# A first weight tile loaded and multiplied in two column halves, and two warm-up products less

## The chip, the cores and the metric

The kernel runs on one core of a Trainium2 chip. The metric is the time of the device for one execution, in microseconds (us). Three runs of the kernel before took 393.03, 393.30 and 393.21 us, median 393.21 us. Beside them there is one profiled execution with its trace.

## The reference

The input x has 2048 tokens of 448 numbers. Three parts are computed from it and mixed:

```python
# attention: 16 heads of 28, each token looks at 8 tokens, 2 apart, itself included
q, k, v = split(x @ wqkv)                       # 448 -> 3 * 448
a = softmax(q . k[s - 2 * (0..7)] * 28 ** -0.5) . v @ wo
# MLP
h = x @ w1 + b1;  h = max(h, 0);  b = (h * h) @ w2 + b2      # 448 -> 1792 -> 448
# gate
g = sigmoid((x * gate_w).sum(-1))
out = g * a + (1 - g) * b
```

All of it is float32. The kernel gets the accuracy on TensorE by splitting each operand into a high part (rounded to the matmul's format, names ending in `h`) and a low part (what the rounding left, names ending in `l`), and adds three products for each pair of tiles: high weights with high x, low weights with high x, and high weights with low x.

## The kernel before, in words

The tokens are worked in four chunks of 512. For each chunk TensorE makes the q, k and v projections (lines 430 to 467), whose 448 input rows are cut into three row tiles of 128 (k = 0, 1, 2) and a rest of 64. A column of the gate vector is appended to q's weights, twice, so that q's weights are 450 columns wide and the gate's sum falls out of the same products. The first hidden tiles of the MLP, the MLP's second product, and the output projection follow on TensorE, while GpSimd and VectorE work on the attention beside it.

The change touches the start of the kernel alone, and one constant of its planner. At the start:

- TensorE runs 18 products with a tile of zeros (`WARM`, line 816), which have no use for the result.
- ScalarE issues the loads of x's first row tile of chunk 0 in two halves of 256 tokens (line 823). SyncE issues all other loads in the order of lines 824 to 838: q's row tile 0 (128 x 450, one transfer, line 826), q's row tile 1, x's row tile 1, q's and x's row tile 2, the rest of q and k in two transfers of 64 rows, x's rest, and then k's and v's weights.
- ScalarE and VectorE make the high and low parts (lines 840 to 858). For k = 0, ScalarE makes the high part of the weights' first 225 columns (line 846) and VectorE that of the other 225 (line 847); VectorE then makes the high part of the first half of x (line 848), the low part of the weights, second half first (line 850), and the low part of x's first half (line 854). x's second half follows (lines 853 and 854).
- `qkv_first` (line 430) makes chunk 0's products. For k = 0 it takes the token tiles 0 and 1 (the first half of x) before the tiles 2 and 3. For each it goes through the three products j = 0 (high with high), 1 (low weights), 2 (low x), so that the first six products of the kernel are: high-high for tiles 0 and 1, low weights for tiles 0 and 1, low x for tiles 0 and 1.

In SBUF the high and low weights of q stand as two blocks of 225 columns, 226 apart. A product reads them woven, one column of each block in turn (`woven`, line 191), so that each product of 450 columns needs both blocks. The order of the columns in the accumulator is undone when ScalarE moves it out (line 373); the gate's column is read on its own (line 379).

What follows the start is written out by a planner. It holds a clock for TensorE (`plan.t`) and for each other engine, and emits each job of ScalarE, VectorE, GpSimd and SyncE in the order in which it expects the job to be able to start. TensorE's clock begins at `START` = 4850 ns (line 861) and is moved on by `FIRST` for the three row tiles of the first products; the other engines' clocks and the due times of the loads after the start are constants that do not depend on `START`.

Of the kernel before, what the change touches and what calls it, by code (L numbers as in the profile page):

```python
# [9 lines left out]
AF = mybir.ActivationFunctionType  # L10
# [3 lines left out]
S, D, H, DH, W, F = 2048, 448, 16, 28, 8, 1792  # L14
# [6 lines left out]
C = HG * DH  # L21
NF = F // P
CH = 512
NQ = D + 2
NH = D // 2 + 1
NG = NH + 1
# [6 lines left out]
MM448, MM512 = 189.2, 216.0  # L33
PE_LAT = 175.0
LAT = 60.0
START = 4850.0
ORDER = (3, 0, 1, 2)
WARM = 18
FIRST = (2700.0, 2350.0, 2300.0)
PP_BUFS = 4  # L40
ST_BUFS = 3
# [6 lines left out]
ACT, DVE, POOL, SYNC = "ACT", "DVE", "POOL", "SP"  # L48
# [8 lines left out]
class Plan:  # L57
# [30 lines left out]
    def add(self, eng, cost, fn, *deps, prio=MID, at=0.0, port=False, move=None):  # L88
        j = Job()
        j.eng, j.cost, j.fn, j.deps, j.prio, j.port, j.move = eng, cost, fn, [d for d in deps if d], prio, port, move  # L90
        j.at, j.done, self.count = max(at, self.now), None, self.count + 1
        j.n = self.count
        self.jobs[eng].append(j)
        return j
# [90 lines left out]
def gated_mix_kernel(ctx: ExitStack, tc: tile.TileContext, xT, wqkv, w1, w2, wo, b1, b2, out):  # L185
    nc = tc.nc
# [4 lines left out]
    def woven(w):  # L191

        if w.shape[1] in (NQ, NQ + 1):
            n = NH if w.shape[1] == NQ else D // 2
            return bass.AP(tensor=w.tensor, offset=w.offset, ap=[list(w.ap)[0], [1, n], [NG, 2]])
        return w.rearrange("p (i n) -> p n i", i=2)
# [9 lines left out]
    def woven_out(pt, n):  # L206
        return (pt[:, :2 * NH] if n == NQ else pt[:, :n]).rearrange("p (n i) -> p n i", i=2)

    def unwoven(t):
        return t.rearrange("p (n i) -> p i n", i=2)  # L210

    plan = Plan()
    add, need, event = plan.add, plan.need, plan.event
# [29 lines left out]
    zt, gt, g1t = zg[:, 0:2], zg[:, 2:4], zg[:, 4:6]  # L243
# [63 lines left out]
    ap = actx.enter_context(tc.tile_pool(name="phase_a", bufs=1, reuse_waits="tile"))  # L307
# [22 lines left out]
    class Acc:  # L330


        def __init__(self, tag, name, n, todo=None, now=True):
            self.ring, self.n, self.tag, self.name = rings[tag], n, tag, name
            self.all = self.todo = todo or 21
            self.rows, self.after = None, tuple(self.ring.take())
            if now:
                need(*self.after)
                self.open()
# [4 lines left out]
    def side_by_side(*todo):  # L344
        assert len(todo[0]) == len(todo[1])
        for pair in zip(*todo):
            need(*(j for e in pair for j in (*e[0].after, *e[3:])))
            for r, (acc, a, w, *_) in enumerate(pair):
                rows = slice(r * 64, r * 64 + 64)
                assert acc.rows in (None, r)  # L350
                nc.tensor.matmul(woven_out(acc.pt, acc.n), a[rows], woven(w[rows]), start=acc.todo == acc.all, stop=acc.todo == 1)  # L351
                acc.todo, acc.rows, acc.after = acc.todo - 1, r, ()
            plan.pe(MM512 if pair[0][0].n == CH else MM448 + (pair[0][0].n - D) * 1.7)

# [7 lines left out]
    def qkv_evacuate(acc, c, tl, b):  # L362
        par, t = c // 2, (c % 2) * 4 + tl
        pt, ready = acc.pt, plan.after_pe()
        first = (b, t // 2) not in stage
        if first:
            stage[b, t // 2] = [None, st_ring.take(), []]
        st = stage[b, t // 2]

        def evacuate():  # L370
            if first:
                st[0] = xap.tile([P, G, 2, C], F32, tag="stage", name=f"st{c}_{tl}_{b}", bufs=ST_BUFS)
            nc.scalar.activation(st[0][:, :, t % 2].rearrange("p (i g) c -> p i g c", i=2),  # L373
                                 unwoven(pt[:, :D]).rearrange("p i (g c) -> p i g c", c=C), AF.Copy)

        jobs = [add(ACT, 540.0, evacuate, ready, *st[1], *st[2], prio=SOON)]
        st[2].append(jobs[0])
        if b == 0:
            jobs.append(add(ACT, 165.0, lambda: nc.scalar.activation(zt[:, par, t:t + 1], pt[:, D + 1:D + 2], AF.Copy),
                            jobs[0], prio=SOON))  # L380
            z_jobs[par].append(jobs[1])
        acc.ring.give(*jobs)
        if not first:
            stage.pop((b, t // 2))
            t0 = t - t % 2
            dst, off = ((q_d, 0), (k_d, HALO), (v_d, HALO))[b]
            dd = dst[par, :, off:off + SP].rearrange("g (p s) c -> p g s c", s=NS)[:, :, t0:t0 + 2]
            j = dma(lambda: nc.sync.dma_start(dd.rearrange("p g s c -> p g (s c)"),
                                              st[0].rearrange("p g s c -> p g (s c)")), 512, 896, *st[2], prio=SOON)
            stores[b, par].append(j)  # L390
            st_ring.give(j)
# [24 lines left out]
    def accs(c, b, tls, tags):  # L416
        return [Acc(t, f"qkv{c}_{tl}_{b}", ncols(b)) for t, tl in zip(tags, tls)]
# [12 lines left out]
    def qkv_first(x):  # L430
        four = range(4)
        q = accs(0, 0, four, "bbbb")
        for k in range(3):
            todo = [full(x, q[i], i, 0, (k,)) for i in four]
            for some in ((0, 1), (2, 3)) if k == 0 else (four,):
                for j in range(3):
                    for i in some:
                        acc, a, w, *_ = todo[i][j]
                        nc.tensor.matmul(woven_out(acc.pt, NQ), a, woven(w), start=k == j == 0, stop=False)  # L439
            plan.pe(FIRST[k])  # L440
        for acc in q:
            acc.todo = 3
        k = accs(0, 1, four, "mmmm")
        t = [sum((last(x, a[i], i, b) for i in four), []) for b, a in ((0, q), (1, k))]
        f = [full(x, k[i], i, 1) for i in four]
        run(0, [t[0] + f[0] + f[1] + f[2] + f[3], t[1] + f[2] + f[3] + f[0] + f[1]],
            [(3, [(0, 0, q[0])], (k[0], k[0])),
             (12, [(0, i, q[i]) for i in (1, 2, 3)], (k[1], k[1])),
             (24, [], (k[0], k[2])), (33, [], (k[1], k[3])),
             (39, [(1, 0, k[0]), (1, 2, k[2])]), (48, [(1, 1, k[1]), (1, 3, k[3])])])  # L450
        v = accs(0, 2, four, "bbbb")
        f, l = [full(x, v[i], i, 2) for i in four], [last(x, v[i], i, 2) for i in four]
        run(0, [f[0] + l[0] + f[2] + l[2] + f[1] + f[3], f[1] + l[1] + f[3] + l[3] + f[0] + f[2]],
            [(15, [], (v[0], v[1])), (24, [], (v[2], v[3])),
             (33, [(2, 0, v[0]), (2, 1, v[1])]), (42, [(2, 2, v[2]), (2, 3, v[3])])])
# [359 lines left out]

    for _ in range(WARM):
        nc.tensor.matmul(warm[:, :2 * P].rearrange("p (i n) -> p i n", i=2), zero, zeros, start=True, stop=True)  # L817

    raws = [rawp.tile([P, 4, 512], F32, tag="raw", name="wqraw0")]
# [3 lines left out]
        nc.scalar.dma_start(rx[:, 0, cols], xT[0, :, 0, cols])  # L823
    for k in range(4):
        if k < 3:
            nc.sync.dma_start(raws[0][:, k, :NQ], wqkv[0, :, k])
        else:
            for b, rows in ((0, slice(0, 64)), (1, slice(64, P))):
                nc.sync.dma_start(raws[0][rows, k, :NQ], wqkv[b, rows, k])
        if k:  # L830
            nc.sync.dma_start(rx[:, k], xT[0, :, k])
    for b, tag in ((1, "k"), (2, "v")):
        raw = attp.tile([P, 3, D], F32, tag=tag, name=f"wqraw{b}")
# [6 lines left out]
    for k in range(3):  # L840
        wh, wl, raw = apart(wqh[:, k]), apart(wql[:, k]), in_a_row(raws[0][:, k])
        if k:
            nc.scalar.activation(wh, raw, AF.Copy)
            nc.vector.tensor_sub(wl, raw, f32(wh))
        else:
            nc.scalar.activation(wh[:, 0], raw[:, 0], AF.Copy)
            nc.vector.tensor_copy(wh[:, 1], raw[:, 1])
            nc.vector.tensor_copy(x.h[0][:, halves[0]], rx[:, 0, halves[0]])
            for i in (1, 0):
                nc.vector.tensor_sub(wl[:, i], raw[:, i], f32(wh[:, i]))  # L850
        for n, cols in enumerate(halves if k == 0 else (slice(0, CH),)):
            if k or n:
                nc.scalar.activation(x.h[k][:, cols], rx[:, k, cols], AF.Copy)
            nc.vector.tensor_sub(x.l[k][:, cols], rx[:, k, cols], f32(x.h[k][:, cols]))
# [5 lines left out]

    plan.t, plan.wire = START, 15000.0
    plan.now = 9800.0
# [119 lines left out]
    c = ORDER[0]  # L982
# [252 lines left out]
    rows = wo_d.rearrange("(i b) n -> i b n", b=14)  # L1235
# [31 lines left out]
    for g in range(2, 2 * NF):  # L1267
        i, f = g // (NF // 2), g % (NF // 2) * 2
        c = ORDER[i]
# [44 lines left out]
        st = at_hand() if last or wo_ready else None  # L1314
# [9 lines left out]
    for n, (tls, second) in enumerate(((left, False), (right, False), (left, True), (right, True))):  # L1324
        if second:
            o_turn(c, f, tls)
        if n in (1, 2, 3):
            st = at_hand()
# [51 lines left out]
```

## Time and profile before

| | us |
|---|---|
| runs: median (lowest, highest) | 393.21 (393.03, 393.30) |
| profiled execution: span from its first to its last instruction | 391.0 |
| median of the runs less this span | 2.2 |
| TensorE products / weight loads busy | 386.5 / 385.2 |
| VectorE / ScalarE / GpSimd busy | 261.4 / 205.4 / 260.6 |
| warm-up products, start of the first to the end of the last | 0.79 to 4.97 |
| first product with data starts | 5.01 |

The profiled execution has no time of its own beside its span; what lies around the span is taken as the difference to the median of the runs, 2.2 us. In the profile, PE is TensorE's products and PEld its weight loads, DVE is VectorE, ACT is ScalarE, POOL is GpSimd and SP is SyncE; a `q` after an engine's name is its queue of issued transfers. In a row of the timeline the first number is the start in us from the span's start, the second the time until the end of the last of the row's instructions; then come engine, line, operation, output <- input, shape and count, and in brackets the idle time of the engine before and what ended it. The names `wqraw` and `xraw` are the loaded float32 tiles of weights and x, `wqh`/`wql` the high and low weights, `qkv` an accumulator in PSUM. The recorded spans of products overlap, since products are pipelined; the distance between starts says how fast they follow one another.

### The profile page before, as it was taken

To read this page: it belongs to the slowest core of one execution; us is meant where nothing else is said; L and a number is where in the kernel's file an instruction comes from. 1 tells how busy PE (TensorE), PEld (TensorE's weight loads), DVE (VectorE), ACT (ScalarE), POOL (GpSimd) and SP (SyncE) were. 2 spreads that over 40 slices of the span, in tenths; PEclk is the share of its full clock that TensorE was granted. 3 is DMA by queue.
4 is the path that set the end of the run, shared out by engine and by line. 5 is a ranking of instruction groups with operands and counts; after the bars stand their busy time and mean duration, and the time that the engine had idled before them with its cause. 6 is when DMAs were issued, how large, how long until landed. Compare 5 with 4: busy or idle time off the path is not lost.

```text
span 391.0 us, 9273 instructions
## 1 busy us (share of the span) xinstructions
PE 386.5 (99%) x3828; PEld 385.2 (99%) x3828; DVE 261.4 (67%) x348; ACT 205.4 (53%) x501; POOL 260.6 (67%) x165
## 2 busy tenths in 40 slices
PE   9999999999999999999999999999999999999996
PEld 8999999999999999999999999999999999999995
DVE  4525523588685778778656989789666686668454
ACT  4757866362566566445555445345716343456740
POOL 0000002988999989959999887999998979661000
PEclk9999999999999999999999999999999999999999
DMA  7999999997174062654203779655635120226835
GB/s 236 400 355 302 382 376 350 378 370 246 49 246 157 1 219 80 220 171 161 90 2 137 242 183 296 208 124 141 213 111 173 78 96 2 88 63 164 143 107 188
DMA packets 64841, 73.75 MB, mean 189 GB/s; under 512 B 32480, under 2 KB 57632, under 8 KB 64416
## 3 DMA queue, kind: packets, MB, share of 16 engines
q1 hardware_dynamic: 64368, 72.79, 57.2%
q8 instruction: 30, 0.49, 0.5%
q10 hardware_dynamic: 432, 0.38, 0.3%
q14 instruction: 11, 0.09, 0.1%
HBM read 45.71 MB, written 28.25 MB: 189 GB/s over the span
## 4 chain that ended last, share of the span: by engine, by line
PE 99%; DVE 0%; DVEq 0%; issue 0%
PE b L351 33%; PE h L351 32%; PE qkv L351 23%; PE a L351 7%; PE qkv L439 2%; PE warm L817 1%; PE a L1170 1%; DVE bt_b L1053 0%; DVEq L1375 0%
## 5 line engine op out<-in xcount | busy, mean ns | idle before, releaser
L549 POOL TENSOR_TENSOR pp<-q,k 128x896 f32<-128x896 f32 x56 | 116.9, 2124 | 75.1 <-DMA k<-k_d 64.4
L561 POOL TENSOR_TENSOR pp<-lg,v 128x896 f32<-128x896 f32 x64 | 113.8, 1870 | 9.6 <-DVE o L571 5.3
L351 PE MATMUL h<-x,w1h 64*128 64x512 f32 x672 | 116.6, 376 | 0.0
L351 PE MATMUL qkv<-wqh,x 64*128 64x448 f32 (+1 forms) x528 | 82.2, 349 | 0.0
L553 DVE TENSOR_REDUCE lg<-pp 128x32 f32<-128x896 f32 x64 | 66.9, 1076 | 13.9 <-POOL pp L549 13.9
L351 PEld LDWEIGHTS h<-x,w1h 64*128 64x128 f32 x672 | 74.1, 186 | 0.0
L803 DVE TENSOR_TENSOR h<-h,h 128x512 fp32r<-128x512 f32 x56 | 38.6, 690 | 52.4 <-ACT h L802 52.3
L351 PE MATMUL h<-x,w1l 64*128 64x512 f32 x336 | 69.3, 376 | 0.0
L351 PE MATMUL b<-w2bh,h 64*128 64x448 f32 x448 | 67.8, 349 | 0.0
L351 PE MATMUL b<-w2ah,h 64*128 64x448 f32 x448 | 67.6, 349 | 0.0
L571 DVE TENSOR_REDUCE o<-pp 128x112 f32<-128x896 f32 x64 | 67.4, 1064 | 0.0
L351 PEld LDWEIGHTS qkv<-wqh,x 64*128 64x128 f32 x528 | 57.3, 186 | 0.0
L799 ACT ACTIVATE h<-h,b1z 128x512 f32<-128x512 f32 x56 | 36.7, 655 | 36.8 <-PE h L351 36.8
L351 PE MATMUL qkv<-wql,x 64*128 64x448 f32 (+1 forms) x264 | 53.4, 349 | 0.0
L351 PEld LDWEIGHTS b<-w2bh,h 64*128 64x128 f32 x448 | 48.0, 192 | 0.0
L351 PEld LDWEIGHTS b<-w2ah,h 64*128 64x128 f32 x448 | 47.9, 193 | 0.0
L351 PE MATMUL b<-w2al,h 64*128 64x448 f32 x224 | 43.2, 349 | 0.0
L351 PE MATMUL b<-w2bl,h 64*128 64x448 f32 x224 | 43.2, 349 | 0.0
L351 PEld LDWEIGHTS h<-x,w1l 64*128 64x128 f32 x336 | 37.4, 186 | 0.0
L801 ACT ACTIVATE h<-h 128x512 fp32r<-128x512 f32 x56 | 33.4, 597 | 1.5
L373 ACT ACTIVATE st<-qkv 128x448 f32<-128x448 f32 x48 | 24.3, 540 | 17.7 <-PE qkv L351 12.9
L802 ACT ACTIVATE h<-h 128x512 f32<-128x512 f32 x56 | 33.1, 592 | 0.0
(111 smaller groups left out, 547.7 us busy)
## 6 DMA issues: line engine op xcount, KB each, us to landing
v<-v_d SPq DMA_DIRECT2D x8, 840.0 KB, 6.0
x_d<-x SPq DMA_DIRECT2D x12, 512.0 KB, 7.3
x<-x_d SPq DMA_DIRECT2D x12, 512.0 KB, 3.5
k<-k_d SPq DMA_DIRECT2D x7, 840.0 KB, 6.5
q_d<-st SPq DMA_DIRECT2D x8, 448.0 KB, 6.1
k_d<-st SPq DMA_DIRECT2D x8, 448.0 KB, 5.8
v_d<-st SPq DMA_DIRECT2D x8, 448.0 KB, 6.2
o_d<-o SPq DMA_DIRECT2D x16, 224.0 KB, 2.2
```

Source lines behind the costliest of these rows:

```text
L351: nc.tensor.matmul(woven_out(acc.pt, acc.n), a[rows], woven(w[rows]), start=acc.todo == acc.all, stop=acc.todo == 1)
L373: nc.scalar.activation(st[0][:, :, t % 2].rearrange("p (i g) c -> p i g c", i=2), unwoven(pt[:, :D]).rearrange("p i (g c) -> p i g c", c=C ...
L439: nc.tensor.matmul(woven_out(acc.pt, NQ), a, woven(w), start=k == j == 0, stop=False)
L549: nc.gpsimd.tensor_mul(pr.rearrange("p (w c) -> p w c", w=W), q[:, s:s + 1].to_broadcast([P, W, C]), k[:, s:s + W])
L553: nc.vector.tensor_reduce(lgs[i][:, s], pr.rearrange("p (w h d) -> p w h d", w=W, h=HG), axis=AX.X, op=ALU.add)
L561: nc.gpsimd.tensor_mul(pr.rearrange("p (h d w) -> p w h d", h=HG, w=W), lgs[i][:, s][:, :, :, None].to_broadcast([P, W, HG, DH]), vs[i][:, ...
L571: nc.vector.tensor_reduce(o_t[par, s][:, g * C:(g + 1) * C], pr.rearrange("p (c w) -> p c w", w=W), axis=AX.X, op=ALU.add)
L799: a = add(ACT, 656.0, lambda pt=pt, r=r: nc.scalar.activation(pt, pt, AF.Relu, bias=b1t[:, f + r:f + r + 1]), ready, *bias_job[:2], prio=NEXT)
L801: b = add(ACT, 600.0, lambda pt=pt, hh=hh: nc.scalar.activation(hh, pt, AF.Square), a, prio=NEXT)
L802: a = add(ACT, 600.0, lambda pt=pt: nc.scalar.activation(pt, pt, AF.Square), b, prio=NEXT)
L803: low = add(DVE, 690.0, lambda pt=pt, hh=hh, hl=hl: nc.vector.tensor_sub(hl, pt, f32(hh)), a, prio=NEXT)
L817: nc.tensor.matmul(warm[:, :2 * P].rearrange("p (i n) -> p i n", i=2), zero, zeros, start=True, stop=True)
```

## The change

- q's row tile 0 is loaded by two transfers of 225 columns each, both issued by SyncE, in place of one of 450. All later transfers of SyncE move one place back.
- The weights' two high halves of k = 0 are both made by ScalarE, one behind the other. VectorE's cast of the second half goes; VectorE begins with x's first half and then makes the low weights, first half first.
- The accumulators of chunk 0's q get another order of columns: two slots of 226, the first from the first 225 weight columns, the second from the other block (each slot weaves the two halves of its block, with one column twice). All of chunk 0's q products are then 452 columns wide in place of 450, and the evacuation and the gate's column are read accordingly.
- For the token tiles 0 and 1, the first product (high-high, k = 0) is made in halves of 226 columns: slot 0 of both tiles, then slot 1 of both.
- `WARM` goes from 18 to 16, and `START` from 4850 to 4450.

```diff
-START = 4850.0
+START = 4450.0
-WARM = 18
+WARM = 16
...
+    HS = NH // 2 + 1
+
+    def in_slots(w, part=None):
+
+        n, o = (2, 0) if part is None else (1, part * NG)
+        return bass.AP(tensor=w.tensor, offset=w[:, o:o + 1].offset, ap=[list(w.ap)[0], [NG, n], [1, HS], [D // 4, 2]])
+
+    def slots_out(pt, part=None):
+        n, o = (2, 0) if part is None else (1, part * 2 * HS)
+        return pt[:, o:o + n * 2 * HS].rearrange("p (s n i) -> p s n i", s=n, i=2)
+
+    def product(acc, a, w, part=None, **kw):
+        if acc.slots:
+            nc.tensor.matmul(slots_out(acc.pt, part), a, in_slots(w, part), **kw)
+        else:
+            nc.tensor.matmul(woven_out(acc.pt, acc.n), a, woven(w), **kw)
...
         def evacuate():
...
+            if acc.slots:
+                nc.scalar.activation(st[0][:, :, t % 2].rearrange("p (s i) c -> p s i c", i=2),
+                                     slots_out(pt).rearrange("p s n i -> p s i n")[:, :, :, :C], AF.Copy)
+                return
...
+            z = 4 * HS - 1 if acc.slots else D + 1
...
     def qkv_first(x):
...
+        for acc in q:
+            acc.slots = True
...
-                    for i in some:
-                        acc, a, w, *_ = todo[i][j]
-                        nc.tensor.matmul(woven_out(acc.pt, NQ), a, woven(w), start=k == j == 0, stop=False)
+                    for part in (0, 1) if k == j == 0 and some == (0, 1) else (None,):
+                        for i in some:
+                            acc, a, w, *_ = todo[i][j]
+                            product(acc, a, w, part, start=k == j == 0 and part != 1, stop=False)
...
-            nc.sync.dma_start(raws[0][:, k, :NQ], wqkv[0, :, k])
+            for cols in (slice(0, NH), slice(NH, NQ)) if k == 0 else (slice(0, NQ),):
+                nc.sync.dma_start(raws[0][:, k, cols], wqkv[0, :, k, cols])
...
-            nc.scalar.activation(wh[:, 0], raw[:, 0], AF.Copy)
-            nc.vector.tensor_copy(wh[:, 1], raw[:, 1])
             nc.vector.tensor_copy(x.h[0][:, halves[0]], rx[:, 0, halves[0]])
-            for i in (1, 0):
+            for i in range(2):
+                nc.scalar.activation(wh[:, i], raw[:, i], AF.Copy)
+            for i in range(2):
                 nc.vector.tensor_sub(wl[:, i], raw[:, i], f32(wh[:, i]))
```

More of the change, by code (lines that the diff above doesn't have):

```diff
@@ L335, in __init__ @@
             self.all = self.todo = todo or 21
-            self.rows, self.after = None, tuple(self.ring.take())
+            self.rows, self.after, self.slots = None, tuple(self.ring.take()), False
             if now:
@@ L350, in side_by_side @@
                 assert acc.rows in (None, r)
-                nc.tensor.matmul(woven_out(acc.pt, acc.n), a[rows], woven(w[rows]), start=acc.todo == acc.all, stop=acc.todo == 1)
+                product(acc, a[rows], w[rows], start=acc.todo == acc.all, stop=acc.todo == 1)
                 acc.todo, acc.rows, acc.after = acc.todo - 1, r, ()
@@ L378, in qkv_evacuate @@
         if b == 0:
-            jobs.append(add(ACT, 165.0, lambda: nc.scalar.activation(zt[:, par, t:t + 1], pt[:, D + 1:D + 2], AF.Copy),
+            z = 4 * HS - 1 if acc.slots else D + 1
+            jobs.append(add(ACT, 165.0, lambda: nc.scalar.activation(zt[:, par, t:t + 1], pt[:, z:z + 1], AF.Copy),
                             jobs[0], prio=SOON))
```

## The prediction

> **What bounds the kernel now.** I read the page first, then the busy time by stretches, then the waits of the weight loads.
>
> ```profile
> span 391.0 us, 9273 instructions
> ...
> PE 99%; DVE 0%; DVEq 0%; issue 0%
> ```
> ```profile
> 0.00:4.97 4.97, 4.18 (x18) 3.92 (x18) 0.65 (x4) 1.68 (x2) 0.80 (x13) 1.00 0.54 160
> 4.97:5.80 0.83, 0.79 (x3) 0.78 (x4) 0.83 (x3) 0.12 (x1) 0.00 (x0) 1.00 1.01 369
> 5.80:12.40 6.60, 6.60 (x37) 6.29 (x35) 4.97 (x9) 5.17 (x10) 0.00 (x0) 1.00 0.99 336
> 12.40:387.30 374.90, 374.88 (x3775) 374.24 (x3774) 254.13 (x332) 198.43 (x490) 259.77 (x152) 1.00 0.58 187
> ```
> ```profile
> PEld warm L817 <- issue: 0.8, 1, 0.8
> PEld qkv L439 <- ACT wqh L846: 0.3, 1, 0.3
> PEld qkv L351 <- issue: 0.3, 1, 0.3
> PEld a L1170 <- issue: 0.3, 1, 0.3
> ```
>
> After each stretch and its length stands the busy time of PE, PEld, DVE, ACT and POOL. From 12.40 to 387.30 us TensorE has 374.88 us of work in 374.90, and the chain that ended last is 99% TensorE. The one wait for another engine is 0.3 us ahead of the first real product; the other two of 0.3 are issue gaps at changes of the array's form, which stay. So everything from the first products on is one solid block, and the change is worth what it moves that block. The decision falls before 6 us:
>
> ```profile
> 0.79 4.18 PE L817 MATMUL warm<-const-float32-0.0 128*128 128x256 f32 x18 [0.79 <-PEq L1372]
> ...
> 4.55 0.42 PE L817 MATMUL warm<-const-float32-0.0 128*128 128x256 f32 x1
> ...
> 5.01 0.71 PE L439 MATMUL qkv<-wqh,x 128*128 128x450 f32 x1
> ...
> 5.51 0.45 PE L439 MATMUL qkv<-wqh,x 128*128 128x450 f32 x1
> 5.79 0.35 PE L439 MATMUL qkv<-wql,x 128*128 128x450 f32 x1
> ...
> 5.99 0.35 PE L439 MATMUL qkv<-wql,x 128*128 128x450 f32 x1
> 6.17 0.35 PE L439 MATMUL qkv<-wqh,x 128*128 128x450 f32 x1
> ...
> 9.21 1.68 PE L439 MATMUL qkv<-wqh,x 128*128 128x450 f32 x8
> ```
>
> Starts tell the rate. Warm-ups follow each other at (4.55 - 0.79) / 17 = 0.221 us for 256 columns, 0.86 ns a column. The eight products at 9.21 follow at (1.68 - 0.35) / 7 = 0.19 us for 450, 0.42 ns a column. So TensorE runs at half rate first, although the granted clock (second last but one column of the stretches) reads 1.00 throughout. The second product starts at 5.51 and makes way at 5.79: 450 columns in 0.28 us fit neither rate. With s us at the slow one, s/0.86 + (0.28 - s)/0.42 = 0.45, s = 0.18: the rate doubles at about 5.69. **This halves the prize**: a product moved from fast to slow time gains only part of what it is moved.
>
> **What holds the first products.**
>
> ```profile
> 4.38 0.39 ACT L846 ACTIVATE wqh<-wqraw 128x225 fp32r<-128x225 f32 x1 [1.43 <-DMA wqraw<-wqkv]
> 5.68 0.42 ACT L853 ACTIVATE x<-xraw 128x256 fp32r<-128x256 f32 x1 [0.91 <-DMA xraw<-xT]
> ```
> ```profile
> 4.38 0.28 DVE L847 CAST wqh<-wqraw 128x225 fp32r<-128x225 f32 x1 [3.52 <-DMA wqraw<-wqkv]
> 4.57 0.28 DVE L848 CAST x<-xraw 128x256 fp32r<-128x256 f32 x1
> 4.77 0.69 DVE L850 TENSOR_TENSOR wql<-wqraw,wqh 128x225 fp32r<-128x225 f32 x2
> 5.38 0.42 DVE L854 TENSOR_TENSOR x<-xraw,x 128x256 fp32r<-128x256 f32 x1
> ```
> ```profile
> 0.76 3.92 PEld L817 LDWEIGHTS warm<-const-float32-0.0 128*128 128x128 f32 x18 [0.76 <-issue]
> 4.97 0.29 PEld L439 LDWEIGHTS qkv<-wqh,x 128*128 128x128 f32 x1 [0.30 <-ACT wqh L846]
> ...
> 5.52 0.28 PEld L439 LDWEIGHTS qkv<-wql,x 128*128 128x128 f32 x1
> ```
>
> The weights land at 4.38. Scalar and vector halves end at 4.77 and 4.66, the cast of x at 4.85, and the first weight load goes at 4.97, 0.12 after the last of them (the profile names ScalarE; VectorE's x was later). The low weights end at 4.77 + 0.69 = 5.46, and their load goes at 5.52, 0.06 after. From load to stream with an idle array: the second product starts 0.50 after the first, 0.39 of it the first's 450 columns, so 0.11 goes ahead of the stream, which begins about 0.15 after the load at 4.97.
>
> **The change part by part.** *Two warm-ups less*: 2 x 0.221 = 0.44 us; the last weight load of a warm-up ends at 4.68 - 0.44 = 4.24. That is room, not gain: it is worth what the data can use.
>
> *The split load.* The trace has no packet of 900 bytes; the nearest rows are the x halves (queue q10, 1024 bytes) and the 1800-byte weight rows that make up q1's packets in the first stretch:
>
> ```profile
> q1 hardware_dynamic: 206, 0.34, 55.8%
> q10 hardware_dynamic: 160, 0.15, 22.0%
> ...
> q1 hardware_dynamic: 192, 0.34, 67.3%
> q10 hardware_dynamic: 128, 0.11, 25.7%
> ```
>
> The first two are 1.7 to 4.0 us, the last two 4.0 to 5.4 (weights and x rows). Share x 16 engines x length / packets: q1 100 and 78 ns, q10 51 and 45 ns. A half of 128 packets at q10's price is 128 x (33 to 49 ns) / 16 = 0.26 to 0.39 us shorter than the whole; I take 0.33, so the **first half lands at 4.05** (bounds: 3.99, and 4.38 if it saves nothing). The second half follows in the same queue, and the second half of x, issued by ScalarE meanwhile, shares the engines with it, as both queues' packets in one stretch show: 256 packets x 45 to 51 ns / 16 = 0.72 to 0.82 us more, so it **lands at 4.80**; without x between, at 4.05 + 0.38 = 4.43; at worst 4.38 + 0.82 = 5.20. I take 4.80, by the rows' mixing. [...]
>
> *The casts.* ScalarE makes high half 0 from 4.05 to 4.44, while VectorE has x by 4.05 + 0.28 = 4.33 (its landing shows no wait of its own now; I take it to come with the weights' half). First load 4.44 + 0.12 = 4.56, 0.41 before 4.97. Stream from 4.71, two halves of 226 columns at 0.86 ns = 0.195 each: done 5.10. High half 1 is ScalarE's now, from 4.80 to 5.19; load 5.31, stream 5.46, up to 5.69 slow and then fast: done 5.77. **The stall that went from the front comes back between the halves**, 5.10 to 5.46. VectorE's low half 1 waits for ScalarE: 5.19 + 0.03 + 0.39 = 5.61, load 5.67, stream 5.82, where it was 5.79: **+0.03**. Next in VectorE's queue is x's low half, 0.42 to about 6.0, for a load that stood at 5.99 and can go at 6.05; its product starts at 6.17 now and at 6.20 then. Beyond, ScalarE's cast of x's second half (5.68, waiting for its transfer) moves to 5.19: no new wait.
>
> *Bounds of this.* Second half at 4.43: high half 1 by 4.83, load 4.95, so the halves run on from 5.10 to 5.49; low half 1 by 5.25. The first low product then runs 5.49 to 5.78 (0.20 slow, the rest fast), the next starts at 5.78 where it was 5.99: **-0.21**. Worst, first half at 4.38 and second at 5.20: high half 1 by 5.59, low by 6.01, stream 6.22: **+0.43**; if the load takes the 0.27 that it took at 5.52, +0.55.
>
> *The halves' own price.* Two loads more, two warm-ups' loads less. A load with a slow product came every 0.221 in the warm-up against 0.195 for a half, so at most 4 x 0.026 = 0.10, inside a stall in my case: nothing.
>
> *452 columns.* 36 products and 6 pairs of the rest, 2 columns each at 0.42 ns: 42 x 0.84 ns = **+0.04**.
>
> *One issue more on SyncE's queue.*
>
> ```profile
> 0.75 0.86 SPq L826 DMA_DIRECT2D wqraw<-wqkv  x2
> ...
> 3.08 1.95 SPq L829 DMA_DIRECT2D wqraw<-wqkv  x2
> ```
> ```profile
> 10.19 0.63 ACT L857 ACTIVATE x<-xraw 128x512 fp32r<-128x512 f32 x1 [0.72 <-DMA xraw<-xT]
> ```
> ```profile
> 10.85 0.69 DVE L858 TENSOR_TENSOR x<-xraw,x 128x512 fp32r<-128x512 f32 x1 [0.68 <-ACT x L857]
> ```
> ```profile
> 12.35 0.46 PE L351 MATMUL qkv<-w7h,x 64*128 64x450 f32 x2
> ...
> 12.83 0.54 PE L351 MATMUL qkv<-w7h,x 64*128 64x450 f32 x4
> ```
>
> An issue is 0.86 / 2 = 0.43 us, and all later ones move back by up to that; the two at 3.08 take 1.95 us in place of 0.9, so the queue already stalls there and swallows some. The latest load that bears on the block is x's rest: high part ready at 10.82 for 12.35, low at 11.54 for 12.83. With 0.45 more, 1.1 and 0.8 us are left. Cost nothing; without that cover, 0.45.
>
> *The sum*: +0.03 + 0.04 = +0.07, span 391.07, and with the 2.2 us around it (393.21 - 391.0) 393.28 us.
>
> **The rivals.** *A, the halves run through* (second half at 4.43, for it: q1 has fewer bytes ahead; against it: q10's packets run in the same stretch): -0.21 + 0.04, **393.04**. Even the full 0.44 of the warm-ups would be 392.8, still no measurable change.
>
> *B, the rate doubles later*, the case on the slower side. The array now pauses 0.30 ahead of the switch at 5.69; then 4.24 to 4.56 and some 0.36 between the halves, 0.68. If what releases the fast rate counts busy time, and from some pause on counts anew, the 4.9 us from 0.79 to 5.69 start again at 4.56 and end at 9.46: 3.77 us at slow rate lose 3.77 x (1 - 0.42/0.86) = 1.93 us, **395.2**. It decides from the first pause that the counting does not forgive, above 0.30 us; for it speaks that work begun at 0.79 took so long to be rewarded, against it that 0.30 was forgiven. [...]
>
> *C, the planner's order.* `START` 0.4 us lower lets evacuations be emitted ahead of loads that were ahead of them. The stretch to 387.30 has 0.02 us free, so nothing can be won there, and a job in the wrong place can cost. For it: all of ScalarE's order after 12 us may move; against it: ScalarE works 198 of 375 us there. Price: one stall like the 0.7 us that ScalarE sat ahead of 10.19 and one as long again, about 1.0: **394.3**.
>
> *D, the split doesn't bring the first half sooner*: the bound above, **393.7 to 393.8**.
>
> **How the numbers follow.** Forecast 0.50, A 0.24, D 0.12, B 0.08, C 0.06. The forecast's own span is 393.1 to 393.5; from A to D without its end, 392.9 to 393.7, is some 0.8. A change of 0.2%, 0.8 us, is about what a measurement of this kernel can tell. Slower: B, half of C, and a little of D with a run's scatter (0.27 us between the three), 0.12. Faster needs more than the 0.44 us there is to win: 0.02. Same: 0.86.
>
> **What would show it.** First load with data at 4.5 to 4.6; second high half on ScalarE at 4.8 behind a wait for its transfer; a second wait of the weight loads of some 0.3, named ScalarE; first low-weight product at 5.8; stretch from 12.4 on still solid. A wait shorter than 0.1 between the halves would show A, products 0.39 apart after 5.8 would show B, an idle PE after 12.4 C. It is wrong if the first low-weight product starts before 5.6 or after 6.3.

## The result and the profile after

The kernel became slower by half a per cent: 395.23 us (median of 13 executions, 393.31 to 396.18) against 393.01 us (13 executions, 392.58 to 393.66); the ratio of the means is 1.0047 with a 95% interval of 1.0035 to 1.0059. The forecast of 393.28 us and its span of 393.1 to 393.5 us, with A to D 392.9 to 393.7, missed it.

The 13 times are not one heap. Five lie at 393.31 to 393.77, eight at 394.86 to 396.18, and none between. The profiled execution is the shortest of them (393.31 us), so its page shows the short group, and nothing of the long one. There the stages stand close to where the prediction put them. From the page of the changed kernel:

```profile
span 391.3 us, 9277 instructions
...
PE 98%; DMA 1%; DVE 0%; ACT 0%; SPq 0%; DVEq 0%; issue 0%
```

Its timeline, TensorE's products, then weight loads, ScalarE and VectorE:

```profile
0.78 3.75 PE L842 MATMUL warm<-const-float32-0.0 128*128 128x256 f32 x16 [0.78 <-PEq L1398]
4.33 0.65 PE L222 MATMUL qkv<-wqh,x 128*128 128x226 f32 x2
5.25 0.74 PE L222 MATMUL qkv<-wqh,x 128*128 128x226 f32 x2 [0.26 <-ACT wqh L874]
5.81 0.57 PE L222 MATMUL qkv<-wql,x 128*128 128x452 f32 x2
6.22 0.93 PE L222 MATMUL qkv<-wqh,x 128*128 128x452 f32 x4
...
4.21 0.50 PEld L222 LDWEIGHTS qkv<-wqh,x 128*128 128x128 f32 x2
5.24 0.50 PEld L222 LDWEIGHTS qkv<-wqh,x 128*128 128x128 f32 x2 [0.53 <-ACT wqh L874]
...
3.64 0.40 ACT L874 ACTIVATE wqh<-wqraw 128x225 fp32r<-128x225 f32 x1 [0.69 <-DMA wqraw<-wqkv]
4.80 0.39 ACT L874 ACTIVATE wqh<-wqraw 128x225 fp32r<-128x225 f32 x1 [0.76 <-DMA wqraw<-wqkv]
...
5.22 0.39 DVE L876 TENSOR_TENSOR wql<-wqraw,wqh 128x225 fp32r<-128x225 f32 x1 [0.76 <-ACT wqh L874]
```

The first half of the weights is used at 3.64 where the whole was used at 4.38, so the first load with data (4.21) waits for nothing. The second half comes at 4.80, and the array waits 0.53 us for it, between the halves. The first low-weight product starts at 5.81, where it was 5.79 before. The start of the whole's last product moved from 386.93 to 387.07 us, 0.14 us later. So this one execution says "no change"; the question is what the eight long ones did.

### The profile page after: what moved, and what is told of

The parts are those of the page before. It is cut to its first block, busy times and chain, and to the rows that moved or that the text cites. A ratio compares the mean times of both kernels' runs of the same rounds, so it can differ in the third digit from the quotient of the medians.

```text
span 391.3 us, 9277 instructions
## 1 busy us (share of the span) xinstructions
PE 386.4 (99%) x3828; PEld 385.0 (98%) x3828; DVE 261.3 (67%) x347; ACT 205.5 (53%) x502; POOL 260.7 (67%) x165
## 4 chain that ended last, share of the span: by engine, by line
PE 98%; DMA 1%; DVE 0%; ACT 0%; SPq 0%; DVEq 0%; issue 0%
PE b L224 32%; PE h L224 32%; PE qkv L224 23%; PE a L224 7%; PE qkv L222 2%; PE a L1196 1%; DMA wqraw<-wqkv 1%; DVE bt_b L1079 0%; ACT wqh L874 0%; SPq L852 0%; DVEq L1401 0%
## 5 line engine op out<-in xcount | busy, mean ns | idle before, releaser
L224 PE MATMUL h<-x,w1h 64*128 64x512 f32 x672 | 121.3, 376 | 0.0
L224 PEld LDWEIGHTS h<-x,w1h 64*128 64x128 f32 x672 | 80.0, 186 | 0.0
L224 PE MATMUL h<-x,w1l 64*128 64x512 f32 x336 | 73.8, 376 | 0.0
L224 PEld LDWEIGHTS qkv<-wqh,x 64*128 64x128 f32 x528 | 60.8, 186 | 0.0
L224 PE MATMUL qkv<-wql,x 64*128 64x448 f32 (+1 forms) x264 | 56.6, 349 | 0.0
L224 PEld LDWEIGHTS b<-w2bh,h 64*128 64x128 f32 x448 | 51.5, 192 | 0.0
L224 PEld LDWEIGHTS b<-w2ah,h 64*128 64x128 f32 x448 | 51.4, 193 | 0.0
L224 PE MATMUL b<-w2bl,h 64*128 64x448 f32 x224 | 46.2, 349 | 0.0
L224 PEld LDWEIGHTS h<-x,w1l 64*128 64x128 f32 x336 | 41.9, 186 | 0.0
L224 PEld LDWEIGHTS qkv<-wql,x 64*128 64x128 f32 x264 | 33.0, 186 | 0.0
```

What stands on the lines that cost most here:

```text
L224: nc.tensor.matmul(woven_out(acc.pt, acc.n), a, woven(w), **kw)
```

## The experiments

A table first. "Release" below is the moment from which products follow each other at the fast rate. "Pause" is the weight loads' wait for data before or between the first products in the profiled execution of that kernel; "long" counts executions over 394.3 us, a bound that I set in the gap of the changed kernel's times; then come the median of the others and the ratio of the means to the kernel before. That kernel stood beside every set: of its 114 executions in five sets 2 were long (394.51 and 395.30 us), the median of the rest is 392.95 us. Its five medians lie at 392.74 to 393.21 us, so differences of some tenths between rows of different sets say little.

| kernel | pause, us | long / all | median of the rest, us | ratio (95%) |
|---|---|---|---|---|
| changed | 0.53 | 8 / 13 | 393.62 | 1.0047 (1.0035 to 1.0059) |
| changed, again | 1.05 | 5 / 12 | 393.56 | 1.0035 (1.0017 to 1.0054) |
| changed, START 4850 | 1.01 | 6 / 9 | 393.72 | 1.0045 (1.0026 to 1.0064) |
| changed, pause filled | 0.23 and 0.22 | 1 / 11 | 393.73 | 1.0019 (1.0005 to 1.0033) |
| changed, 18 warm-ups | 0.56 | 3 / 12 | 393.48 | 1.0027 (1.0013 to 1.0041) |
| changed, x's half later | 0.74 and 0.48 | 4 / 12 | 393.43 | 1.0027 (1.0012 to 1.0041) |
| changed, x's half on SyncE | 0.19, later 1.93 | 4 / 6 | 394.02 | 1.0039 (1.0027 to 1.0052) |
| changed, one load | 0.74 | 4 / 12 | 392.83 | 1.0018 (1.0003 to 1.0033) |
| changed, one load, 18 warm-ups | 0.28 | 0 / 12 | 393.10 | 1.0001 (0.9991 to 1.0010) |
| before, 16 warm-ups | 0.73 | 1 / 12 | 392.81 | 0.9999 (0.9985 to 1.0013) |
| before, 14 warm-ups | 1.07 | 5 / 12 | 392.77 | 1.0021 (1.0007 to 1.0036) |
| before, 8 warm-ups | 2.67 | 5 / 5 | none | 1.0051 (1.0038 to 1.0064) |
| before, split load only | 1.32 | 2 / 11 | 393.71 | 1.0026 (1.0014 to 1.0038) |

**The changed kernel again**, unchanged.

> The changed kernel unchanged, to see how its executions spread and, if the profile falls on a long one, where its time lies. Theory R (the fast rate of the products is released later in some executions, because the array pauses 0.53 us between the halves): times in two groups, near 393.5 and near 395.5, and in a long one the products of the first row tiles 0.38 us apart for some 3 to 4 us more than in a short one, with everything behind them shifted by the same 1.7 to 2 us. Theory P (the planner's order, START): the loss lies in waits behind 12.5 us, and the products before it stand as in the short execution. Theory S (the second half of the weights lands late in some executions): the second high half stands 1.5 us or more later than at 4.80.

Two groups again, 393.34 to 393.99 and 395.27 to 395.73 us. The profile fell on the longest of the short ones (393.99). From its timeline, ScalarE and then TensorE:

```profile
3.68 0.39 ACT L874 ACTIVATE wqh<-wqraw 128x225 fp32r<-128x225 f32 x1 [0.73 <-DMA wqraw<-wqkv]
5.21 0.39 ACT L874 ACTIVATE wqh<-wqraw 128x225 fp32r<-128x225 f32 x1 [1.14 <-DMA wqraw<-wqkv]
...
4.33 0.45 PE L222 MATMUL qkv<-wqh,x 128*128 128x226 f32 x2
5.65 0.48 PE L222 MATMUL qkv<-wqh,x 128*128 128x226 f32 x2 [0.87 <-ACT wqh L874]
6.08 0.65 PE L222 MATMUL qkv<-wql,x 128*128 128x452 f32 x2
```

The second half lands at 5.21, not at 4.80, and the pause is 1.05 us. Yet at the halves nothing more is lost: the second halves are done at the fast rate (5.65 to 6.08 with the load of the next), and the first low-weight product is 0.27 us later than in the profile above. The fast rate had already been released when the pause came: the first two halves take 0.45 us in all, the same pair took 0.65 in the profile above. Row tile 1's x is late as well, cast at 7.72 where it was at 6.88 above, and the array waits for it once more:

```profile
8.40 0.68 PEld L222 LDWEIGHTS qkv<-wqh,x 128*128 128x128 f32 x4 [0.49 <-ACT x L879]
```

With both, the last product starts 0.75 us later than in the profile above (387.82 for 387.07). So late data alone cost some tenths at each place, and the moment of the release differs between executions.

**START put back.**

```diff
-START = 4450.0
+START = 4850.0
```

> The changed kernel with START put back to 4850, so that the planner's clock stands as before. Theory R: still two groups, median 395 within 0.5 unless the share of the groups shifts by chance. Theory P: 393.0 to 393.6 in all executions. Theory S: as R.

Six of nine are long, so `START`, and the order that the planner makes of it, is not the cause. This time the profile is a long execution (395.88 us). Its products:

```profile
4.33 0.70 PE L222 MATMUL qkv<-wqh,x 128*128 128x226 f32 x2
5.77 0.77 PE L222 MATMUL qkv<-wqh,x 128*128 128x226 f32 x2 [0.74 <-ACT wqh L874]
6.33 0.98 PE L222 MATMUL qkv<-wql,x 128*128 128x452 f32 x2
7.11 1.71 PE L222 MATMUL qkv<-wqh,x 128*128 128x452 f32 x4
8.62 0.96 PE L222 MATMUL qkv<-wql,x 128*128 128x452 f32 x2
9.37 1.69 PE L222 MATMUL qkv<-wqh,x 128*128 128x452 f32 x6
10.90 0.93 PE L222 MATMUL qkv<-wql,x 128*128 128x452 f32 x4
11.67 1.51 PE L222 MATMUL qkv<-wqh,x 128*128 128x452 f32 x7
```

The four products from 7.11 to 8.62 follow 0.38 us apart, double the 0.19 of the four from 10.90 to 11.67. The six from 9.37 to 10.90 took 1.53 where 1.14 would be fast, so two more of them were slow: the release came near 10.1 us, not near 5.7. Against the short execution, the first low-weight product is 0.52 late (6.33 for 5.81), and 3.8 us more at the slow rate lose 3.8 x (1 - 0.19/0.38) = 1.9. With a wait of 0.4 us far later, which this profile has alone, that adds up to 2.8 us; its last product is 2.75 us late (389.82 for 387.07).

**Only the warm-ups, before's loads and products.**

```diff
-WARM = 18
+WARM = 16
```

> The kernel before with 16 warm-up products in place of 18 and nothing else; the real products start when their data are there, so the pause ahead of them grows from 0.30 to 0.74 us. Theory R: the pause is longer than the 0.53 us of the changed kernel, so most executions lose 1.7 to 2 us, median 394.7 to 395.2. Theories P and S: nothing changes, 393.0 within 0.3, since neither START nor the load is touched.

My theory was wrong here in its size: a pause of 0.73 us was harmless in 11 of 12 executions, and the median is before's (0.9999). So two warm-ups less cost nothing by themselves that these 12 executions can tell. With 14 the pause reaches 1.1 us:

```diff
-WARM = 18
+WARM = 14
```

> The kernel before with 14 warm-up products: no split, same data times, the pause ahead of the first real product 1.17 us (0.30 before, 0.73 with 16, which cost nothing in 10 of 12 executions). Theory R with a tolerance between 0.53 (the short execution of the changed kernel) and 1.01 (the long one with START 4850): more than half of the executions at 394.0 to 395.5, the rest near 392.7. Rival S alone (only the late second half costs; the pause as such is harmless): all within 392.5 to 393.4.

Now five are over 394.3 and two more at 394.15 and 394.17, while the other five stay at 392.58 to 393.17 as if nothing had been done. There is no split in this kernel, and its data are on time. From its profile, a long execution (394.32 us):

```profile
4.91 1.09 PE L439 MATMUL qkv<-wqh,x 128*128 128x450 f32 x2 [0.80 <-DVE x L848]
5.79 0.96 PE L439 MATMUL qkv<-wql,x 128*128 128x450 f32 x2
6.54 1.71 PE L439 MATMUL qkv<-wqh,x 128*128 128x450 f32 x4
8.04 0.96 PE L439 MATMUL qkv<-wql,x 128*128 128x450 f32 x2
8.79 1.36 PE L439 MATMUL qkv<-wqh,x 128*128 128x450 f32 x6
9.99 0.92 PE L439 MATMUL qkv<-wql,x 128*128 128x450 f32 x4
```

The first products start as early as before (4.91 and 5.79 against 5.01 and 5.79); from 6.54 they are 0.38 apart, until about 8.9. With this a pause without any split is shown to put off the release, in some executions and not in others. Fewer warm-ups also leave less work ahead of the pause, and this run does not part the two; in the run with the pause filled, further down, the warm-ups stay as they are.

**A long pause**, to ask how the release is counted:

```diff
-WARM = 18
+WARM = 8
```

> The kernel before with 8 warm-up products: they end near 2.6, the array pauses some 2.4 us until the first real product at 5.0. [...] Theory R as a count of busy time that starts anew after the pause (4.9 us from 5.0): all executions near 395.0 within 0.3. Theory without release: 392.6 to 393.4.

The five times are 394.38, 394.53, 394.76, 395.25 and 395.33 us: all long, and 0.95 us apart, where I had put a count that starts anew with the first product within 0.3. By the rates, 0.95 us of time would be 1.9 us of difference in the release. But the kernel before spreads by 1.2 us and more itself, so the scatter alone does not decide. In the profile (394.53 us) the products fall to 0.19 apart near 9.0:

```profile
5.24 1.09 PE L439 MATMUL qkv<-wqh,x 128*128 128x450 f32 x2 [2.41 <-DVE x L848]
6.12 0.96 PE L439 MATMUL qkv<-wql,x 128*128 128x450 f32 x2
6.87 1.71 PE L439 MATMUL qkv<-wqh,x 128*128 128x450 f32 x4
8.37 0.84 PE L439 MATMUL qkv<-wql,x 128*128 128x450 f32 x2
9.05 1.30 PE L439 MATMUL qkv<-wqh,x 128*128 128x450 f32 x6
```

That is 3.8 us after the restart, less than the 4.9 us that my rival B counted. In the four profiles of long executions with a late release it came 3.8 us (here), 4.0 (14 warm-ups), 4.3 (START 4850) and 4.4 us (the change without the split load, further down) after the restart: no one figure, so no plain count. What the release waits for no run shows; the profile's granted clock reads 1.00 in slow stretches too (START 4850: 1.00 from 6.33 to 14.20 us, with products at half the rate until near 10.1).

**The pause filled**: two products of zeros between the first and second halves.

```diff
                     for part in (0, 1) if k == j == 0 and some == (0, 1) else (None,):
+                        if part == 1:
+                            for _ in range(2):
+                                nc.tensor.matmul(warm[:, :2 * P].rearrange("p (i n) -> p i n", i=2), zero, zeros, start=True, stop=True)
```

> The changed kernel with two products of zeros (256 columns, 0.22 us each) put between the first and the second halves, which fill most of the 0.53 us pause and wait for nothing. Theory R: the long executions go, all within 392.5 to 393.7, median 393.2. Theory P: as the changed kernel, median 395. Theory S: as the changed kernel, since the second half's landing is not touched.

As theory R had it for the long group: one execution of eleven is left (395.78 us), against 19 of 34 of the changed kernel, its repeat and it with START 4850. The warm-ups are the same 16, so it is the idle time between the halves that makes the difference. But the rest did not come down to 393.2. It stays at 393.47 to 394.19 us, some 0.8 above the kernel before. That part of the loss has another cause, which the next runs find.

**18 warm-ups with the split.**

```diff
-WARM = 16
+WARM = 18
```

> The changed kernel with 18 warm-up products: the first halves start 0.44 us later (4.65 to 4.8), so the pause ahead of the second halves shrinks from 0.5 to 1.05 us to 0.1 to 0.6; the second half's landing stays. Theory R: at most 2 in 10 executions over 394.5, the rest at 393.2 to 393.9, median 393.6. Rival S alone: the share of long executions stays near a half, median 394 to 395.

Three of twelve are long, and the rest is where it was (393.48). The share fell, though not quite to what I wrote, and 3 of 12 against 19 of 34 is no sure difference; the profiled execution's second half came at 5.23, and 0.56 us of pause were left.

**The split load alone** in the kernel before; casts, products and 18 warm-ups are untouched.

```diff
-            nc.sync.dma_start(raws[0][:, k, :NQ], wqkv[0, :, k])
+            for cols in (slice(0, NH), slice(NH, NQ)) if k == 0 else (slice(0, NQ),):
+                nc.sync.dma_start(raws[0][:, k, cols], wqkv[0, :, k, cols])
```

> The kernel before with only q's first row tile loaded as two transfers; casts, products and 18 warm-ups as before, so the first product needs both halves. Theory R+S: second half at 4.8 to 5.3, the first real product at 5.4 to 5.9, pause 0.8 to 1.2 us; 0.2 to 0.5 us lost in every execution, and about a half of them 1.7 us more: two groups near 393.4 and 395.2. If the split load by itself is harmless: 393.0 within 0.3 in all executions.

Nine of eleven at 393.23 to 394.24, median of the rest 393.71: 0.76 us over the kernel before's 392.95. The split load alone carries a loss as large as the one that the filled pause left. I expected a half of the executions in the long group and saw two after a wait of 1.32 us. Its profile, ScalarE, VectorE and TensorE:

```profile
3.67 0.39 ACT L847 ACTIVATE wqh<-wqraw 128x225 fp32r<-128x225 f32 x1 [0.71 <-DMA wqraw<-wqkv]
...
5.24 0.28 DVE L848 CAST wqh<-wqraw 128x225 fp32r<-128x225 f32 x1 [4.37 <-DMA wqraw<-wqkv]
...
5.86 0.62 PE L439 MATMUL qkv<-wqh,x 128*128 128x450 f32 x2 [1.16 <-ACT x L854]
```

The halves come at 3.67 and 5.24; the whole came at 4.38. Half of the weights is 0.7 us earlier and the other half 0.9 us later. The pause did no more harm in this execution because the release was ahead of it:

```profile
0.78 3.92 PE L817 MATMUL warm<-const-float32-0.0 128*128 128x256 f32 x18 [0.78 <-PEq L1373]
```

The same 18 warm-ups took 4.18 us in the profile of the kernel before, so here the last of them ran at the fast rate already.

**The converse: all of the change but the split load.**

```diff
-            for cols in (slice(0, NH), slice(NH, NQ)) if k == 0 else (slice(0, NQ),):
-                nc.sync.dma_start(raws[0][:, k, cols], wqkv[0, :, k, cols])
+            nc.sync.dma_start(raws[0][:, k, :NQ], wqkv[0, :, k])
```

> The changed kernel with q's first row tile loaded as one transfer again; halves of products, casts on ScalarE, 16 warm-ups and START as changed. Whole weights at 4.38, high halves at 4.77 and 5.07, first halves at 4.9, second at 5.2 to 5.3 without a pause, low weights at 5.5, first low-weight product at 5.6 to 5.75. Theory R+S: pause 0.65 us ahead of the halves and none between: times as the kernel before, median 392.7 to 393.1, at most 2 in 10 over 394.3. Theory P (order, or the 452 columns and halves by themselves cost): median 393.4 or more.

The rest's median is 392.83 us, 0.09 above the kernel before of this set, so the 0.7 us go with the split load, and halves, 452 columns and planner cost nothing that can be measured. Four of twelve are long, more than the "2 in 10" that I wrote. The pause is that of 16 warm-ups (0.74), which had made 1 of 12 long with whole products. The profile is a long one (394.80 us):

```profile
5.01 1.17 PE L222 MATMUL qkv<-wqh,x 128*128 128x226 f32 x4 [0.47 <-DVE x L871]
...
6.75 1.71 PE L222 MATMUL qkv<-wqh,x 128*128 128x452 f32 x4
...
9.01 1.54 PE L222 MATMUL qkv<-wqh,x 128*128 128x452 f32 x6
10.39 0.93 PE L222 MATMUL qkv<-wql,x 128*128 128x452 f32 x4
```

The six products from 9.01 to 10.39 took 1.38 where 1.15 would be fast, so about one of them was slow still: the release comes near 9.4, 4.4 us after the first product. The next run asks whether the halves are to blame:

```diff
-WARM = 16
+WARM = 18
```

> The run before last again (halves of products, whole load) with 18 warm-up products, so that the pause ahead of the first halves is 0.30 us as in the kernel before in place of 0.74. Theory R: the 4 of 12 executions near 394.9 go, at most 1 in 12 over 394.3; the rest stays at 392.7 to 393.3. Rival (halves of 226 columns do not keep the array busy enough to be released, whatever the pause): 3 to 5 of 12 stay near 394.9.

None of twelve is long; ratio 1.0001. With the short pause the halves do no harm. Whether they add to a pause of 0.74 us stays open, since 4 of 12 against 1 of 12 is too little to tell. The products run on without a wait between the halves:

```profile
4.97 0.67 PE L222 MATMUL qkv<-wqh,x 128*128 128x226 f32 x4
5.54 0.65 PE L222 MATMUL qkv<-wql,x 128*128 128x452 f32 x2
6.03 0.93 PE L222 MATMUL qkv<-wqh,x 128*128 128x452 f32 x4
```

**What delays the second half**: x's second half taken from ScalarE's queue and issued by SyncE behind it.

```diff
-    for cols in halves:
-        nc.scalar.dma_start(rx[:, 0, cols], xT[0, :, 0, cols])
+    nc.scalar.dma_start(rx[:, 0, halves[0]], xT[0, :, 0, halves[0]])
...
                 nc.sync.dma_start(raws[0][:, k, cols], wqkv[0, :, k, cols])
+            if k == 0:
+                nc.sync.dma_start(rx[:, 0, halves[1]], xT[0, :, 0, halves[1]])
```

> The changed kernel with one transfer moved: the second half of x's first row tile is issued by SyncE behind the second half of the weights in place of by ScalarE beside it. Theory R+S (the second half of the weights lands at 4.8 to 5.3 because x's second half shares the engines with it, the array pauses 0.5 to 1.0 us for it, and a pause of that length makes executions miss the release of the fast rate): the second half lands at 4.1 to 4.5, the pause falls under 0.3 us, no execution near 395.5, and the first low-weight product starts near 5.4 in place of 5.8: median 392.5 to 392.9, at or below the kernel before. Rival: a 900-byte half is slow by itself: lands at 4.8 or later, two groups as in the changed kernel.

Half of it came true. ScalarE casts both halves in a row, the products run on, and the first low-weight product starts at 5.15, 0.66 us sooner:

```profile
3.84 0.83 ACT L875 ACTIVATE wqh<-wqraw 128x225 fp32r<-128x225 f32 x2 [1.37 <-DMA wqraw<-wqkv]
4.91 0.42 ACT L880 ACTIVATE x<-xraw 128x256 fp32r<-128x256 f32 x1 [0.23 <-DMA xraw<-xT]
6.74 0.58 ACT L870 ACTIVATE wqh<-wqraw 128x450 fp32r<-128x450 f32 x1 [1.42 <-DMA wqraw<-wqkv]
8.24 0.63 ACT L880 ACTIVATE x<-xraw 128x512 fp32r<-128x512 f32 x1 [0.92 <-DMA xraw<-xT]
...
4.46 0.78 PE L222 MATMUL qkv<-wqh,x 128*128 128x226 f32 x4
5.15 0.65 PE L222 MATMUL qkv<-wql,x 128*128 128x452 f32 x2
...
8.92 1.03 PE L222 MATMUL qkv<-wqh,x 128*128 128x452 f32 x4 [1.58 <-ACT x L880]
9.79 0.93 PE L222 MATMUL qkv<-wql,x 128*128 128x452 f32 x4
10.56 1.70 PE L222 MATMUL qkv<-wqh,x 128*128 128x452 f32 x8
```

So it was x's second half beside it that held the second half back: cast at 4.28 in this profile, at 4.80 to 5.33 in the seven profiles of this study with the split and x's half beside. But row tile 1 then comes late: its weights are cast at 6.74 (5.91 in the changed kernel) and its x at 8.24 (6.88), and TensorE waits 1.93 us for them. All six executions are at 393.97 to 395.47 us, without a gap between groups; what was won was lost one transfer later. The profiled one counts as long in the table (394.62 us), but by this wait and not by a late release: the four products from 9.79 to 10.56 follow 0.19 us apart. Once released, a pause of 1.9 us did not end the fast rate.

I then tried to delay x's half only a little, by an activation of one element between ScalarE's two issues:

```diff
     nc.scalar.dma_start(rx[:, 0, halves[0]], xT[0, :, 0, halves[0]])
+    nc.scalar.activation(b1z[0:1, 14:15], none, AF.Copy)
+    nc.scalar.dma_start(rx[:, 0, halves[1]], xT[0, :, 0, halves[1]])
```

> The changed kernel with the second half of x's first row tile issued by ScalarE only behind its table load (at 3.1 in place of 1.2), by a one-element activation put between its two issues. Theory R+S: the second half of the weights has the engines nearly to itself and is used at 4.1 to 4.5 as in the run with x's half on SyncE (4.24), the halves of the products run on without a pause, the first low-weight product starts at 5.1 to 5.4; x's second half lands at 5.3 to 5.8, in time for its products at 5.9 to 6.0 or up to 0.3 late, and row tile 1 is not pushed back by it. Median 392.5 to 393.0, no execution over 394.5. Rival (what is won at the halves is lost at row tile 1 again, as with x's half on SyncE): weight loads wait 0.5 us or more for row tile 1 and the median is 393.3 to 394.5.

The edit didn't do what it was for. The second issue stands at 1.24, while the table load ran:

```profile
0.74 0.41 ACTq L847 DMA_DIRECT2D xraw<-xT  x1
1.18 1.28 ACT L848 ACT_TABLE_LOAD   x1 [1.18 <-PEq L1399]
1.24 0.39 ACTq L849 DMA_DIRECT2D xraw<-xT  x1
```

Its times are those of the changed kernel (393.43 for the rest, 4 of 12 long), and it tells nothing of a later x. No kernel of this study beats the kernel before; the two that equal it are 16 warm-ups alone and the change without the split load and with 18 warm-ups.

## Why the prediction was wrong

*The bound* was right in the profiled execution: one solid block of TensorE from the first products on, and nothing but its start counts. In the second profile of the same kernel a wait of 0.49 us for row tile 1's x stands at 8.40, inside the block.

*The half rate* was right in kind and wrong in one assumption. I worked out 5.69 us for the release from one execution and then used it as if it belonged to the kernel. It belongs to the execution: in the profiles it lies anywhere from ahead of 4.4 us (the changed kernel again, by its first halves) to about 6 in short executions and at 8.9 to 10.1 in the four long ones with a late release. A small error beside it: the 0.86 ns a column has the step from the first warm-up to the second in its mean (0.35 us, the others 0.21); without it the slow rate is 0.83, just double the fast one.

*The first half at 4.05* came sooner, at 3.64 (3.64 to 4.40 in the seven profiles with the split and x's half beside it). *The second at 4.80* was met to the hundredth in the profiled execution, but in the other six of these it came at 5.18 to 5.33, about the worst bound that I gave (5.20). **This term was mis-sized**: the likely +0.03 should have been the +0.43, and with the 0.04 of the columns and what the later transfers lose the short group is 0.6 to 0.8 us above the kernel before, as the runs with and without the split load show from both sides (393.71 and 392.83). That was rival D, in all but its first half. No profile with x's half beside it came near the favourable end that I gave, 4.43: the second half came 0.42 us later than the whole's 4.38 in the profiled execution and 0.8 to 0.95 us later in those six.

*The stall between the halves* was forecast, though too small (some 0.3 us against a measured wait of 0.53 to 1.05), and priced only by its own length. **This is the step that failed**: that the pause costs what it lasts. In 19 of 34 executions (the changed kernel's two sets and START 4850) it put off the release as well, which costs some 2 us; that is read from the times, and in the one of the 19 that was profiled, from its products. It is rival B in kind. That its 395.2 us is the measured median is luck: B had every execution long, and the median fell there because 8 of 13 were; with 5 of 12 in the second set it is 393.85. I gave it 0.08, on the ground that 0.30 us had been forgiven. The right question was how much more than 0.30 the pauses would be, and 0.68 by my own sum is more than double. Its mechanism needs a correction: not a count of 4.9 us that begins anew (the release came 3.8 to 4.4 us after the restart), and hardly a fixed limit on the pause, since 0.73 us was harmless in a short profile (16 warm-ups) and 0.74 stands in a long one (the change without the split load). The pause itself differs between executions, 0.53 to 1.05 us in two profiles of one kernel, so a part of the two groups may come from that. What decides it from one execution to the next was not seen. The shares differ more than I can explain (2 of 11 with the split load alone and a wait of 1.32 us, 19 of 34 with the change). A pause behind the release did not bring the slow rate back where a profile shows one (1.93 us with x's half on SyncE, 1.05 and 0.49 us in the changed kernel again), so the work ahead of the pause may bear on the share as much as its length: 18 warm-ups and 1.32 us gave 2 of 11, 14 and 1.07 us 5 to 7 of 12. These two kernels differ in their loads too, so that stays open.

*The halves' own price* (nothing) and *rival C* (START put back changes nothing) stood. *The warm-ups* were no gain, as forecast, but not free to drop either: with 14 five to seven of 12 executions lose some 2 us. *SyncE's extra issue* was priced at nothing by x's rest alone; row tile 1's x, which the sum did not look at, kept TensorE waiting for 0.49 us in one profile. Whether that comes from the later issue or from the transfers ahead of it is not shown. *Rival A* was never reached: where the halves did run through with the split load, row tile 1 was late.

## What to carry to other kernels

Here, work that came in earlier at the start of the kernel was paid for by other transfers of the same moment: with x's half on SyncE the second half of the weights was cast 0.5 us earlier than in the changed kernel (4.28 for 4.80) and row tile 1's weights 0.8 us later (6.74 for 5.91), its x 0.5 to 1.4 us later (8.24 for 6.88, and 7.72 in the repeat). So look at what lands next, and price the last piece to arrive, not the first. If the trace shows that an engine starts slow and speeds up later, a pause before that point may be priced twice: its own length (here 0.53 to 1.05 us), and the chance that the speed-up is missed (here some 2 us in 19 of 34 executions). And one profiled execution tells one draw; where several times of a kernel are at hand, look at whether they form one group before reading a mean or a median from them.

## What was not expected of the hardware

- Pauses of 0.5 to 1.1 us in the first 6 us, ahead of the release, put off TensorE's fast rate in some executions and not in others of the same kernel, with 2 us between the groups; a pause of 1.93 us after the release did not bring the slow rate back (products 0.19 us apart from 9.79 on).
- The granted clock reads 1.00 in stretches where products follow at half the rate (START 4850: 0.38 us apart from 7.11 to 8.62 in place of 0.19, the clock 1.00 from 6.33 to 14.20); the distance between their starts shows it.
- Splitting a 225 KB load in two brought its first half to use 0.3 to 0.7 us earlier (in six of seven profiles) and its second 0.4 to 0.95 us later than the whole, with another queue's 128 KB load beside it. The whole was used at 4.29 to 4.61 in five profiles.
- ScalarE's queue issued a transfer at 1.24 us that stands behind an activation in kernel.py, while that activation's table load ran from 1.18 to 2.46.
